# A fused attention and feed-forward kernel on one core: the first weight piece issued by ScalarE, two warm-up matmuls fewer, and re-timed tiles

## The chip, the core and the metric

The kernel runs on one core of one Trainium2 chip. The core has five engines that run side by side, each with its own stream of instructions: TensorE (PE in the profile; its weight loads are shown as PEld), VectorE (DVE), ScalarE (ACT), GpSimd (POOL) and SyncE (SP), which issues most transfers. They wait for each other through semaphores. The metric is device time in microseconds of one execution; several executions are measured and their median is taken.

## The reference

Both halves work on the same x (1 x 2048 x 640, bf16). A is a linear attention with 32 heads of 20; its feature map is a softmax of a small per-head product and of its negative. B is a gated feed-forward net with 1728 hidden columns. A sigmoid gate mixes them.

```python
g = sigmoid((x * gate_w).sum(-1, keepdims=True))
q, k, v = split(x @ wqkv)                       # 32 heads of 20
pq, pk = q @ w_phi, k @ w_phi                   # per head
phi_q = concat([softmax(pq), softmax(-pq)])     # 40 features
phi_k = concat([softmax(pk), softmax(-pk)])
kv, z = phi_k.T @ v, phi_k.sum(over tokens)
a = ((phi_q @ kv) / (phi_q @ z + 1e-6)) @ wo
b = (silu(x @ w_gate) * (x @ w_up)) @ w_down
out = g * a + (1 - g) * b
```

## The kernel before

Everything stays in on-chip memory between load and store. Tokens are handled in four blocks of 512 for the gate and up products and in 16 tiles of 128 for keys, queries and outputs. Products over the 640 input columns are five matmuls of 128 rows each, accumulated in one of eight PSUM banks. x is brought in transposed, by transposing transfers (`load_x`), block by block; block 0 comes in three pieces (columns 0-1, 2-3 and 4 of the five 128-column groups).

The order of work is not written out by hand. Each piece of work is a task for one engine with a cost, dependencies, a priority and the PSUM banks and buffers that it takes (`_Plan.add`). `_Plan.run` (line 286) plays the tasks against the costs and emits the instructions of each engine in the order found; the chip then runs this fixed order, and waits wherever the real times differ. Two sorts of constants steer it:

- `land` in `load` (line 490): the time at which a transfer is taken to have landed. A task that needs it is not placed before that time. Loads of one issuing engine are chained, so that each engine's queue keeps its order.
- `start.hold` (line 880): the earliest planned start of each key tile (`K_AT + K_EACH * t`) and query tile (`Q_AT + Q_EACH * t`). `PRE_Q` is the priority of the products that fold w_phi into the query weights, `D_AFTER` the number of gate-and-up pairs of a block that come ahead of the first down product of the block before.

The start is laid out apart. `warm` (line 614) issues matmuls on a constant into PSUM banks, ten in two groups; nothing reads their results. Behind them `ffn_head` (line 688) computes the first four of the 14 column groups of gate and up for block 0 in pieces, as weights and x arrive: gate over x groups 0-1 for the four column groups (8 matmuls), up over the same (8), then gate and up over x groups 2-4 (12 each). `load_head` (line 537) loads the weight pieces for this. All these loads and the transposing loads of x are issued by SP, one behind the other, beginning with w_gate's piece of two groups by 512 columns. ACT issues one transfer, gate_w, behind its second Tanh; it starts with the load of its function table, ahead of a one-element Tanh.

A key tile runs its products on PE, max, min and two subtractions on DVE, Exp on ACT, sum and reciprocal on DVE and the scaling on POOL. A query tile runs the same and then a transposing transfer, the products with kv, the division on DVE, a second transposing transfer and the product with wo. Gate and up need Tanh and a copy on ACT, one operation on DVE and one on POOL for each column group.

Of the kernel before, what the change touches and what calls it, by code (L numbers as in the profile page):

```python
# [6 lines left out]
P = 128  # L7
# [33 lines left out]
class _Tracker:  # L41
# [123 lines left out]
    def run(self, eng, fn, reads=(), writes=(), semname=None, inc=None):  # L165
        rkeys = [self._key_of(a) for a in reads]
        wkeys = [self._key_of(a) for a in writes]
        need = {}

        def req(ev):  # L170
            if ev is None:
                return
            s, v = ev
            if v > need.get(s, 0):
                need[s] = v

        for k in rkeys:
            for kk in self._conflicts(k):
                req(self.lastw[kk])
        for k in wkeys:  # L180
            for kk in self._conflicts(k):
                req(self.lastw[kk])
                for s, v in self.readers[kk].items():
                    req((s, v))
        self._emit_waits(eng, need)
        ins = fn()
        if semname is None:
            semname = {"pe": "pe", "act": "act", "dve": "dve", "pool": "pool"}[eng]
            if inc is None:
                inc = 1  # L190
        elif semname == "dma":
            semname = self.new_dma_sem()
            inc = 16
        ins.then_inc(self.sem[semname], inc)
        self.cnt[semname] += inc
        v = self.cnt[semname]
        ev = (semname, v)
        snapd = dict(self.known[eng])
        if snapd.get(semname, 0) < v:
            snapd[semname] = v  # L200
        self.evknow.setdefault(semname, {})[v] = snapd
        for k in wkeys:
            self.lastw[k] = ev
            self.readers[k] = {}
        for k in rkeys:
            r = self.readers[k]
            if r.get(semname, 0) < v:
                r[semname] = v
        return ev
# [31 lines left out]
class _Plan:  # L241
# [11 lines left out]
    def add(self, eng, cost, fn, deps=(), prio=5.0, lat=None, acq=(), rel=(), name=""):  # L253
        t = _Task(eng, cost, fn, deps, prio, self.LAT[eng] if lat is None else lat,
                  tuple(acq), tuple(rel), len(self.tasks), name)
        self.tasks.append(t)
        return t
# [86 lines left out]
def _build(  # L344
# [13 lines left out]
    pe, act, dve, pool, sp = nc.tensor, nc.scalar, nc.vector, nc.gpsimd, nc.sync  # L358
# [67 lines left out]
    def one(b, c0, c1, r0=0, r1=P):  # L426
        return ps[r0:r1, b * 512 + c0:b * 512 + c1]
# [42 lines left out]
    def dma(eng, dst, src, transpose=False, keep=False):  # L470
        eobj = tr.engobj[eng]
        reads = [src] if src.tensor.name in tr.addr else []
        writes = [dst] if dst.tensor.name in tr.addr else []
        fn = (lambda: eobj.dma_start(dst, src, transpose=True)) if transpose else (lambda: eobj.dma_start(dst, src))
        ev = run(eng, fn, reads=reads, writes=writes, semname="dma")
        if keep:
            out_evs.append(ev)
# [12 lines left out]
    def load(eng, dst, src, land, prio, transpose=False, name="load", cost=0.06):  # L490

        t = add(eng, cost, lambda: dma(eng, dst, src, transpose=transpose), prio=prio, lat=2.0, name=name)
        t.land = land
        t.slack = L_SLACK if land > 13 else 0.0
        t.after = chain.get(eng)
        chain[eng] = t
        return t
# [7 lines left out]
    wgl = [None] * (NPC + 1)  # L505
    wul = [None] * (NPC + 1)

    def load_gu(j, eng, land, prio):
        c0, c1 = PIECES[j]
        wgl[j] = load(eng, wg[:, :, c0:c1], gsrc[:, :, c0:c1], land[0], prio)  # L510
        wul[j] = load(eng, wu[:, :, c0:c1], usrc[:, :, c0:c1], land[1], prio + 0.1)

    def load_x(bt, prio, *cuts):

        tok = slice(512 * bt, 512 * bt + 512)
        out_ = []
        for i, (c0, c1, land) in enumerate(cuts):
            out_ += [load("sp", xT[:, c0:c1, tok], x2[tok, c0 * P:c1 * P], land, prio + 0.1 * i, True, "x%d" % bt)] * (c1 - c0)
        return out_
# [13 lines left out]
    xs = [None] * NBT  # L533
    HD = 4
    hw = {}

    def load_head(key, c0, c1, k0, k1, land, prio):
        w, src = (wg, gsrc) if key == "g" else (wu, usrc)
        t = load("sp", w[:, c0:c1, k0 * P:k1 * P], src[:, c0:c1, k0 * P:k1 * P], land, prio)
        for k in range(k0, k1):  # L540
            hw[key, c0, k] = t
        return t
    load_head("g", 0, 2, 0, HD, 3.9, -43)
    xa = load_x(0, -42, (0, 2, 5.25))
    load_head("u", 0, 2, 0, HD, 6.9, -41)
    load_head("g", 2, 5, 0, 2, 7.4, -40.5)
    xs[0] = xa + load_x(0, -40, (2, 4, 8.8), (4, 5, 9.3))
    wgl[0] = load_head("g", 2, 5, 2, HD, 10.0, -39.5)
    wul[0] = load_head("u", 2, 5, 0, HD, 11.3, -39)
    load_gu(1, "sp", (12.5, 13.7), -37)  # L550
    xs[1] = load_x(1, -36.5, (0, 5, 16.4))
    phi_rows = A_w_phi.rearrange("h e f -> (h e) f")
# [61 lines left out]
    def warm(banks, before):  # L614
        ctx = {}

        def fn():
            for b in banks:
                last = pe.matmul(one(b, 0, 512), lhsT=ones_row[:, 0:P], rhs=ones_row[:, 0:512], start=True, stop=True, skip_group_check=True)  # L619
            return last  # L620
        b0, b1 = min(banks), max(banks) + 1
        t = add("pe", 0.427 * len(banks), lambda: run("pe", fn, reads=[], writes=[ps[:, b0 * 512:b1 * 512]]), prio=-10,
                acq=[("bank", ctx, i) for i in range(b0, b1)], rel=[("bank", ctx, i) for i in range(b0, b1)], name="warm")
        t.after = before
        return t
    warm_t = warm((4, 5, 6, 7, 4, 5), warm((0, 1, 2, 3), None))


    gate_t = {}
# [85 lines left out]
            ffn_tail(0, k, cs[k], (last["g", k], last["u", k]), 0)  # L715

    B_FIRST = 8
    K_AT, K_EACH, Q_AT, Q_EACH = 29.00, 6.158, 120.27, 8.184
    PRE_Q = 10.11
    PRE_EACH = 2.3  # L720
    PRE_AT = 23.6
    D_AFTER = 5
    FIN_DVE = 12
    K_PAIRS = 9
    store_t = {}
# [64 lines left out]
    def premult(which, wT_l, prio, step=0.0, at=0.0):  # L790
        ev = []
        for m in range(5):
            ctx = {}

            def fn(m=m, ctx=ctx):
                i = ctx["ps"]

                def piece(c, o_, n):
                    k_ = PC if n == PC else P
                    return (o_, wqT[0:k_, NPC_W * which + c, P * m:P * m + P],  # L800
                            wbd[0:k_, c, 0:n // DH, :].rearrange("p k f -> p (k f)"), True, True)
                mms([piece(c, bank(i, 0, 32 + PC * c, 32 + PC * c + PC), PC) for c in range(4)] +
                    [piece(4, bank(i, 1, 0, PC), PC), piece(5, bank(i, 1, PC, PC + 2 * DH), 2 * DH)])
            t1 = add("pe", 0.285, fn, deps=wT_l + wbd_t, prio=prio + step * m, acq=[("pair", ctx, "ps")], name="pre")
            t1.hold = at + PRE_EACH * m if at else 0.0

            def ev_fn(m=m, ctx=ctx):
                i_ = wide(ctx["ps"], 32 + D)[:, 32:32 + D]
                o_ = wkv[:, m, 0:D] if which else wq[:, m, :]
                if which and m % 2:  # L810
                    dveop(lambda: dve.tensor_copy(o_, i_), [i_], [o_])
                else:
                    actop(o_, i_, ACTF.Copy)
            ev.append(add("dve" if which and m % 2 else "act", 0.73 if which and m % 2 else 0.6, ev_fn, deps=[t1], prio=-1,
                          rel=[("pair", ctx, "ps")], name="prev"))
        return ev
# [225 lines left out]
    pre_k = premult(1, wkT_l, 2.0, at=PRE_AT)  # L1042
    pre_q = premult(0, wqT_l, PRE_Q, 0.02)
    wq_done[0] = pre_q[-1]
# [8 lines left out]
    for bt in range(1, NBT):  # L1053
        ks = list(range(K_PAIRS if bt == 1 else 0, NK))
        ds = [("d", u, bt - 1) for u in range(4)]
        for i, k in enumerate(ks):
            seq.append(("f", k, bt))
            if i >= D_AFTER and ds:
                seq.append(ds.pop(0))
# [21 lines left out]
def bass_gated_mix__linear_kernel_hedgehog__swiglu_ffn__prompt_kernel(  # L1081
    nc: bass.Bass,
    A_x: bass.AP,
    A_wqkv: bass.AP,
    A_w_phi: bass.AP,
    A_wo: bass.AP,
    B_x: bass.AP,
    B_w_gate: bass.AP,
    B_w_up: bass.AP,
    B_w_down: bass.AP,  # L1090
    gate_w: bass.AP,
    out: bass.AP,
):
    with nc.Block() as block:
        @block.gpsimd
        def _(g):
            _build(nc, A_x, A_wqkv, A_w_phi, A_wo, B_x, B_w_gate, B_w_up, B_w_down, gate_w, out)
# [29 lines left out]
```

## Time and profile before

| What | us |
|---|---|
| Median of 3 runs (lowest, highest) | 286.96 (286.87, 287.4) |
| The profiled execution | 287.4 |
| Its span, first to last instruction | 285.7 |
| PE busy | 282.5 |
| DVE busy | 223.4 |
| POOL busy | 171.6 |
| ACT busy | 149.1 |
| Transfers, share of 16 DMA engines over the span | 40.1% |

The span is shorter than the execution's time; 1.7 us lie around it. Matmuls are pipelined, and their ends are modelled: one of 512 columns is shown with some 380 ns, while the next starts 216 ns after it. So PE's pace is read from starts, not from lengths. DMA shares are means over short windows and can exceed 1 where packets overlap.

### The profile page before, as it was taken

Reading aid. Unit: us, or ns where it says so; the run is one execution under the profiler, and the core shown is the slowest. Engines: PE = TensorE matmul, PEld = TensorE weight load, DVE = VectorE, ACT = ScalarE, POOL = GpSimd, SP = SyncE. Lnnn points to the kernel's source line nnn. Section 1 sums busy time; section 2 is a strip of 40 time slices with the busy share of each in tenths; the row PEclk is TensorE's granted clock in tenths of the full one; section 3 lists DMA queues with packets and bytes.
Section 4 is the critical chain, followed back from the end, with each engine's and each line's share of the span. In section 5 each row is a group of like instructions: output and inputs, shape, how many; then the busy total and the mean of one; then the engine's idle time right before and its main releaser. Section 6 shows DMA issues by size and latency. Waiting matters only on the chain.

```text
span 285.7 us, 5001 instructions
## 1 busy us (share of the span) xinstructions
PE 282.5 (99%) x1970; PEld 149.6 (52%) x1970; DVE 223.4 (78%) x318; ACT 149.1 (52%) x238; POOL 171.6 (60%) x168
## 2 busy tenths in 40 slices
PE   8999999999999999999999999999999999999996
PEld 3445554555554555654455656555554555555654
DVE  1323449998999797799999999999979979962312
ACT  2455655886676564436636444566664653562210
POOL 5099633749478635456784485589898458638100
PEclk9999999999999999999999999999999999999999
DMA  7979997920000000000002483744375245363211
GB/s 171 271 120 246 214 245 129 334 86 0 0 2 0 0 2 0 2 0 2 0 2 52 76 125 77 109 112 94 69 144 70 55 83 118 70 76 73 71 46 46
DMA packets 68112, 24.22 MB, mean 85 GB/s; under 512 B 56249, under 2 KB 68089, under 8 KB 68089
## 3 DMA queue, kind: packets, MB, share of 16 engines
q1 hardware_dynamic: 67433, 23.91, 40.1%
q8 instruction: 15, 0.25, 0.4%
q10 hardware_dynamic: 656, 0.00, 0.1%
q14 instruction: 8, 0.07, 0.1%
HBM read 8.30 MB, written 2.62 MB: 38 GB/s over the span
## 4 chain that ended last, share of the span: by engine, by line
PE 99%; DVE 0%; issue 0%
PE ps L446 97%; PE ps L619 2%; DVE xsb L749 0%
## 5 line engine op out<-in xcount | busy, mean ns | idle before, releaser
L665 POOL TENSOR_TENSOR hT<-hT,us 128x512 bf16<-128x512 bf16 (+1 forms) x56 | 64.1, 1154 | 53.1 <-DVE hT L659 31.1
L932 POOL TENSOR_TENSOR phi<-phi,rc 128x1320 bf16<-128x1320 bf16 x32 | 77.6, 2426 | 28.8 <-DVE rc L926 26.0
L446 PE MATMUL ps<-xT,wg 128*128 128x512 bf16 x280 | 69.7, 381 | 0.0
L446 PE MATMUL ps<-xT,wu 128*128 128x512 bf16 x260 | 64.3, 379 | 0.0
L446 PE MATMUL ps<-wd,hT 128*128 128x512 bf16 (+1 forms) x448 | 63.0, 299 | 0.0
L922 DVE TENSOR_REDUCE sm<-phi 128x66 f32<-128x1320 bf16 x32 | 48.5, 1519 | 10.6 <-ACT phi L456 10.6
L659 DVE SCALAR_TENSOR_TENSOR hT<-hT,ps 128x512 bf16<-128x512 bf16 (+1 forms) x56 | 37.6, 676 | 22.8 <-ACT hT L456 22.7
L456 ACT ACTIVATE hT<-ps 128x512 bf16<-128x512 f32 (+1 forms) x56 | 33.2, 597 | 40.7 <-PE ps L446 40.3
L456 ACT ACTIVATE phi<-phi 128x1320 bf16<-128x1320 bf16 x32 | 41.7, 1304 | 22.2 <-DVE phi L911 22.2
L446 PEld LDWEIGHTS ps<-wd,hT 128*128 128x128 bf16 x448 | 35.0, 98 | 27.4
L446 PE MATMUL ps<-wkv,xT 128*128 128x289 bf16 (+2 forms) x240 | 45.8, 343 | 0.0
L456 ACT ACTIVATE us<-ps 128x512 bf16<-128x512 f32 (+1 forms) x56 | 33.2, 597 | 16.4 <-PE ps L446 14.2
L446 PEld LDWEIGHTS ps<-xT,wu 128*128 128x128 bf16 x260 | 25.3, 98 | 30.8 <-ACT phi L456 0.4
L446 PEld LDWEIGHTS ps<-xT,wg 128*128 128x128 bf16 x280 | 26.0, 98 | 27.9 <-issue 1.5
L446 PEld LDWEIGHTS ps<-wkv,xT 128*128 128x128 bf16 x240 | 22.9, 97 | 18.4
L899 DVE TENSOR_REDUCE mx<-ps 128x33 f32<-128x660 f32 x32 | 26.6, 833 | 3.4 <-PE ps L446 3.3
L911 DVE TENSOR_TENSOR phi<-mn,ps 128x660 bf16<-128x660 f32 x32 | 26.4, 824 | 0.3
L903 DVE TENSOR_REDUCE mn<-ps 128x33 f32<-128x660 f32 x32 | 26.5, 828 | 0.0
L907 DVE TENSOR_TENSOR phi<-ps,mx 128x660 bf16<-128x660 f32 x32 | 26.5, 827 | 0.0
L456 ACT ACTIVATE xsb<-ps,gs 128x640 bf16<-128x640 f32 x16 | 12.7, 793 | 24.7 <-PE ps L446 24.7
L446 PE MATMUL ps<-wq,xT 128*128 128x512 bf16 (+1 forms) x160 | 24.3, 299 | 0.0
L446 PE MATMUL ps<-wo,oT 128*128 128x512 bf16 (+1 forms) x160 | 24.3, 299 | 0.0
(47 smaller groups left out, 184.9 us busy)
## 6 DMA issues: line engine op xcount, KB each, us to landing
out_dram<-xsb SPq DMA_DIRECT2D x15, 160.0 KB, 1.8
wd<-in_B_w_down_dram SPq DMA_DIRECT2D x1, 2080.0 KB, 9.3
wg<-in_B_w_gate_dram SPq DMA_DIRECT2D x2, 400.0 KB, 5.3
wu<-in_B_w_up_dram SPq DMA_DIRECT2D x2, 400.0 KB, 6.5
wo<-in_A_wo_dram SPq DMA_DIRECT2D x1, 800.0 KB, 10.0
wg<-in_B_w_gate_dram SPq DMA_DIRECT2D x2, 320.0 KB, 4.7
wu<-in_B_w_up_dram SPq DMA_DIRECT2D x2, 320.0 KB, 5.6
wkv<-in_A_wqkv_dram SPq DMA_DIRECT2D x1, 600.0 KB, 4.4
```

The source lines that it names most:

```text
L446: last = pe.matmul(o, lhsT=l, rhs=r, start=st, stop=sp_, skip_group_check=True)
L456: run("act", lambda: act.activation(o, i, func, scale=scale), reads=reads, writes=[o])
L619: last = pe.matmul(one(b, 0, 512), lhsT=ones_row[:, 0:P], rhs=ones_row[:, 0:512], start=True, stop=True, skip_group_check=True)
L659: dveop(lambda: dve.scalar_tensor_tensor(out=hap, in0=hap, scalar=1.0, in1=g_, op0=ALU.add, op1=ALU.mult), [hap, g_], [hap])
L665: poolop(lambda: pool.tensor_tensor(hap, hap, u_, ALU.mult), [hap, u_], [hap])
L899: dveop(lambda: dve.tensor_reduce(a, b, AX.X, ALU.max), [b], [a])
L903: dveop(lambda: dve.tensor_reduce(a, b, AX.X, ALU.min), [b], [a])
L907: dveop(lambda: dve.tensor_tensor(o_, a, b, ALU.subtract), [a, mx[:, ctx["st"], :]], [o_])
L911: dveop(lambda: dve.tensor_tensor(o_, a, b, ALU.subtract), [b, mn[:, ctx["st"], :]], [o_])
L922: dveop(lambda: dve.tensor_reduce(a, b, AX.X, ALU.add), [b], [a])
L932: poolop(lambda: pool.tensor_tensor(a, a, b, ALU.mult), [a, r], [a])
```

## The change

The first piece of w_gate is issued by ACT and no longer by SP, through a new argument of `load_head`. SP's queue then begins with the first piece of x. The planned landing times of the head's pieces become smaller. The second group of warm-up matmuls has four in place of six. Five constants of the planned order are changed: key tiles are planned 0.05 us further apart, query tiles start 1.25 us earlier and lie 0.097 us closer, `PRE_Q` goes from 10.11 to 10.14 and `D_AFTER` from 5 to 4. No computation of the result is changed.

```diff
-    def load_head(key, c0, c1, k0, k1, land, prio):
+    def load_head(key, c0, c1, k0, k1, land, prio, eng="sp"):
         w, src = (wg, gsrc) if key == "g" else (wu, usrc)
-        t = load("sp", w[:, c0:c1, k0 * P:k1 * P], src[:, c0:c1, k0 * P:k1 * P], land, prio)
+        t = load(eng, w[:, c0:c1, k0 * P:k1 * P], src[:, c0:c1, k0 * P:k1 * P], land, prio)
         for k in range(k0, k1):
             hw[key, c0, k] = t
         return t
-    load_head("g", 0, 2, 0, HD, 3.9, -43)
-    xa = load_x(0, -42, (0, 2, 5.25))
-    load_head("u", 0, 2, 0, HD, 6.9, -41)
-    load_head("g", 2, 5, 0, 2, 7.4, -40.5)
-    xs[0] = xa + load_x(0, -40, (2, 4, 8.8), (4, 5, 9.3))
-    wgl[0] = load_head("g", 2, 5, 2, HD, 10.0, -39.5)
-    wul[0] = load_head("u", 2, 5, 0, HD, 11.3, -39)
+    load_head("g", 0, 2, 0, HD, 3.9, -43, "act")
+    xa = load_x(0, -42, (0, 2, 4.6))
+    load_head("u", 0, 2, 0, HD, 6.2, -41)
+    load_head("g", 2, 5, 0, 2, 6.9, -40.5)
+    xs[0] = xa + load_x(0, -40, (2, 4, 8.0), (4, 5, 8.5))
+    wgl[0] = load_head("g", 2, 5, 2, HD, 9.6, -39.5)
+    wul[0] = load_head("u", 2, 5, 0, HD, 10.9, -39)
...
-    warm_t = warm((4, 5, 6, 7, 4, 5), warm((0, 1, 2, 3), None))
+    warm_t = warm((4, 5, 6, 7), warm((0, 1, 2, 3), None))
...
-    K_AT, K_EACH, Q_AT, Q_EACH = 29.00, 6.158, 120.27, 8.184
-    PRE_Q = 10.11
+    K_AT, K_EACH, Q_AT, Q_EACH = 29.00, 6.208, 119.02, 8.087
+    PRE_Q = 10.14
...
-    D_AFTER = 5
+    D_AFTER = 4
```

## The prediction

> **What bounds the kernel now.** I read the page's busy shares first, then the chain of work that ended last.
>
> ```profile
> PE 282.5 (99%) x1970; PEld 149.6 (52%) x1970; DVE 223.4 (78%) x318; ACT 149.1 (52%) x238; POOL 171.6 (60%) x168
> ...
> PE ps L446 97%; PE ps L619 2%; DVE xsb L749 0%
> ```
>
> TensorE (PE) is busy for 99% of the span, and the chain is PE nearly from end to end. A busy PE need not be a PE at its pace, so next I looked at the starts of single matmuls. In the steady part a 512-column matmul starts 0.216 us after the one before it, and that pace is hardly ever broken. The largest break I found is this one:
>
> ```profile
> 137.34 1.03 PE L446 MATMUL ps<-xT,wg 128*128 128x512 bf16 x4
> 138.25 0.59 PE L446 MATMUL ps<-xT,wu 128*128 128x512 bf16 x2
> ```
>
> Four matmuls at 0.216 from 137.34 end at 138.20; the next begins at 138.25, 0.05 late. The excess over the pace, summed over all starts from 6.34 on, is about 0.2 us. So the end is set by three things: when PE begins useful work, at which pace it runs there, and whether anything makes it wait later. Third view, the timeline of the first microseconds (start, length, engine) of SyncE (SP), of PE and of PE's weight loads (PEld), which mark single matmul starts:
>
> ```profile
> 0.80 0.46 SPq L474 DMA_DIRECT2D wg<-in_B_w_gate_dram  x1
> 1.32 1.32 SPq L474 DMA_TRANSPOSE xT<-in_A_x_dram  x1
> 2.70 0.56 SPq L474 DMA_DIRECT2D wu<-in_B_w_up_dram  x1
> ```
>
> ```profile
> 0.84 4.43 PE L619 MATMUL ps<-const-bfloat16-1.0 128*128 128x512 bf16 x10 [0.84 <-PEq L1111]
> 5.08 2.50 PE L446 MATMUL ps<-xT,wg 128*128 128x512 bf16 x8
> 7.42 1.89 PE L446 MATMUL ps<-xT,wu 128*128 128x512 bf16 x8
> ```
>
> ```profile
> 5.05 0.16 PEld L446 LDWEIGHTS ps<-xT,wg 128*128 128x128 bf16 x2 [0.69 <-issue]
> 5.49 0.15 PEld L446 LDWEIGHTS ps<-xT,wg 128*128 128x128 bf16 x1 [0.28 <-issue]
> 5.92 0.15 PEld L446 LDWEIGHTS ps<-xT,wg 128*128 128x128 bf16 x1 [0.28 <-issue]
> 6.34 0.75 PEld L446 LDWEIGHTS ps<-xT,wg 128*128 128x128 bf16 x4 [0.27 <-issue]
> ```
>
> Ten warm-up matmuls cover 0.84 to 5.06; the first useful one starts at 5.08. Up to 6.34 starts lie 0.427 us apart, after it 0.216: the clock turns at about 6.33. The views of transfers (median us from issue to landing) and of ScalarE (ACT) for the same stretch:
>
> ```profile
> wg<-in_B_w_gate_dram SPq DMA_DIRECT2D x1, 256.0 KB, 3.0
> xT<-in_A_x_dram SPq DMA_TRANSPOSE x1, 3.6
> ```
>
> ```profile
> 0.80 1.28 ACT L456 ACT_TABLE_LOAD   x1 [0.80 <-PEq L1111]
> ...
> 10.64 0.60 ACT L456 ACTIVATE hT<-ps 128x512 bf16<-128x512 f32 x1 [8.34 <-PE ps L446]
> ```
>
> The first piece of x lands at 1.32 + 3.6 = 4.9, just ahead of 5.05; w_gate lands at 0.80 + 3.0 = 3.8.
>
> **The change, part by part.**
>
> *Warm-ups.* Two of ten go, so PE is free at 0.84 + 8 x 0.424 = 4.23 (ten took 4.24). From there it waits for x and w_gate, if they are not there.
>
> *Issue.* ACT issues w_gate's piece at 0.80; its cost is 0.46 (SP's row). ACT's table load moves from 0.80 to 1.26 and its first Tanh from 2.09 to about 2.55, hidden under the 8.34 us in which ACT waits for PE up to 10.64; without that cover it would cost 0.46. SP issues x at 0.80, not 1.32, and what follows on SP's queue moves up by up to 0.52. Both transfers now run side by side. Windows of the trace (columns: window, length, busy time of each engine with counts, clock, DMA share, GB/s):
>
> ```profile
> 1.80:3.10 1.30, 1.30 (x5) 0.46 (x4) 0.68 (x3) 0.49 (x2) 1.09 (x5) 1.00 0.73 195
> 3.10:3.90 0.80, 0.80 (x4) 0.27 (x2) 0.54 (x2) 0.00 (x0) 0.70 (x3) 1.00 1.19 240
> ```
>
> The DMA engines have room only up to 3.1 (share 0.73). So x lands between 0.52 earlier (all of the issue time) and not earlier (the same 512 KB through the same full engines), and w_gate no later than the pair together, 4.9. I take 0.40: nearer the full value, because the room lies where x's packets would now begin. PE's first useful matmul is then at 5.08 - 0.40 = 4.68. The Trainium skill, DMA: Bandwidth & Descriptors, "Issuing engines are not separate DMA queues", says that issuing from several engines saves only the sequencer's issue time, since the same 16 engines move everything. By it the gain is at most the 0.52 and may be nothing, which is rival B; the DMA shares above agree.
>
> *What an earlier start is worth.* The clock turns at a time, 6.33, and what PE does ahead of it runs at half pace: 1 us more gives 1/0.427 = 2.34 matmuls, each of which saves 0.216 later, 0.51 us. So 0.40 x 0.51 = -0.20. Bounds: 0, and -0.43 (two matmuls at 0.216) if both transfers were there at 4.23.
>
> *The rest of the head.* w_up's piece lands at 2.70 + 3.3 = 6.0 and is needed at 7.42 - 0.20 = 7.22; the second and third piece of x land at 8.0 and 8.5 by their semaphores and are needed 0.20 before 9.15 and 10.01. Even if none came earlier, they have about 1 us; with that gone PE would wait microsecond for microsecond. Cost nothing.
>
> *The order behind.* K_EACH, Q_AT, Q_EACH, PRE_Q and D_AFTER move the planned starts. The order of the built program shows the same work on each engine, apart from the two matmuls and the moved issue, but PE, VectorE (DVE), ACT and SyncE come in another order from the first key tiles on. The work costs nothing; the waits are redrawn. From below: the 0.2 us of excess goes. From above, VectorE: it is full where the query tiles run (same columns; the third busy time is DVE's):
>
> ```profile
> 121.00:150.00 29.00, 29.00 (x215) 15.12 (x214) 28.79 (x40) 13.96 (x23) 20.77 (x17) 1.00 0.01 1
> 150.00:200.00 50.00, 50.00 (x389) 27.57 (x388) 49.12 (x74) 27.35 (x34) 33.97 (x29) 1.00 0.50 92
> ```
>
> Query tiles are planned 8.184 - 8.087 = 0.097 closer; if DVE takes none of that and PE waits for it each time, 16 x 0.097 = +1.55. I take +0.20: four breaks of the size of the one at 138.25, nearer the lower bound because PE's waits now end that close to the pace, and the new order has no more work to place.
>
> *The end* is as before: the last stores follow the last matmul in the same order, 283.3 to 285.7.
>
> Sum: -0.20 + 0.20 = 0.0. The span stays 285.7 and its execution 287.4 (1.7 lies around the span). That execution is the slowest of the three shown, 0.44 above their median of 286.96, so the forecast is **287.0**. 0.2%, 0.57 us, is about what a measurement of this kernel can tell from no change.
>
> **Rivals.**
>
> A, faster: the clock turns before the useful matmuls start, and each microsecond counts in full. x lands 0.52 earlier, the 0.2 of excess shrinks to 0.1: 286.96 - 0.52 - 0.1 = 286.3. For it: the other runs are 0.44 and 0.53 faster than the profiled one, as a clock that turns 1 us earlier would make them (1 x 0.51). Against it: in the one execution that shows the clock it turned 1.25 us after the first useful start.
>
> B, the change doesn't do what it says: x lands at 4.9 as before. PE idles from 4.23, nothing is gained, the redrawn waits stay: 287.2.
>
> C, slower, at one place: the hole in PE's work from 4.23 to 4.68 makes the clock begin anew. Before, the clock turned 6.33 - 0.84 = 5.49 after the first matmul, with no hole. Counted from 4.68 it turns at 10.17, and PE runs 3.84 us longer at half pace: 3.84 x 0.51 = +1.9, so 288.9. It decides as soon as the granted clock turns after about 6.4. For it: the one turn that the trace shows came with no hole ahead of it. Against it: the hole is 0.45 of 5.49 us. The Trainium skill, TensorE: Matmul & The Clock Gate, "Part 1", names a free-running window of about 3.4 us that must be busy; by it a hole could cost at most one window, an estimated 3.4 x 0.51 = 1.7 us. No row here shows how much idleness is allowed.
>
> D, slower: DVE sets the pace among the query tiles. Ten of the 16 at 0.097 cost 1.0: 288.0. For it: 28.79 busy of 29.00. Against it: DVE has no more work than before, and has 43 - 39.5 = 3.5 us free between 200 and 243.
>
> **Chances.** The forecast (286.6 to 287.4) 0.36, A 0.25, B 0.09, C 0.13, D 0.17. The range 286.3 to 288.1 leaves out C and the lower quarter of A, about 0.19. Faster by over 0.2%: most of A (0.22) and the forecast's edge (0.03), 0.25. Slower: C, most of D (0.15) and the other edge (0.03), 0.31. Within: 0.44.
>
> **What would show it.** Eight warm-ups ending at 4.23; x landing near 4.5 and the first useful matmul near 4.7 (5.08 shows B); the change from 0.427 to 0.216 near 6.3 (10 shows C, below 4.7 shows A); then four cold useful matmuls in place of three; the steady pace with about 0.4 us of breaks in all (1 us or more, with PE released by DVE between 120 and 245, shows D). A landing of w_up after 7.2, or a tail over 2.4 us, would be a miss that no case holds.

## The result, and the profile after

| | Before | After |
|---|---|---|
| Median of 22 runs each, us | 287.10 | 287.66 |
| Lowest, highest | 286.71, 287.65 | 287.33, 289.56 |
| Mean | 287.11 | 287.89 |
| The profiled execution | 287.4 | 289.38 |
| Its span | 285.7 | 287.7 |

The ratio after to before is 1.0026, with an interval of 1.0016 to 1.0037: slower, by about what such a measurement can tell. The means are 0.78 apart and the medians 0.56. The 22 runs after are not one heap. Nineteen lie between 287.33 and 287.98, with a mean of 287.65; three lie at 289.27, 289.38 and 289.56. The profiled execution is one of these three, so its profile shows a loss that most executions don't have. The two parts have to be read apart.

The page of the kernel after, first the busy time of each engine, then the shares of the chain of waits by engine and by line:

```profile
PE 283.6 (99%) x1968; PEld 149.6 (52%) x1968; DVE 224.1 (78%) x318; ACT 150.3 (52%) x238; POOL 171.5 (60%) x168
...
PE 96%; DMA 1%; ACT 1%; DVE 0%; issue 0%
PE ps L446 96%; DMA xT<-in_A_x_dram 1%; ACT phi L456 0%; ACT hT L456 0%; ACT us L456 0%; DVE xsb L749 0%
```

PE still shows 99%. New on the chain are a transfer of x at its head, and ACT with 1%. The head comes first: the timelines of SP, of PE and of PE's weight loads (start, length, engine, line, what was done).

```profile
0.80 1.33 SPq L474 DMA_TRANSPOSE xT<-in_A_x_dram  x1
2.19 0.57 SPq L474 DMA_DIRECT2D wu<-in_B_w_up_dram  x1
```

```profile
0.84 3.57 PE L619 MATMUL ps<-const-bfloat16-1.0 128*128 128x512 bf16 x8 [0.84 <-PEq L1111]
5.21 3.57 PE L446 MATMUL ps<-xT,wg 128*128 128x512 bf16 x8 [0.79 <-DMA xT<-in_A_x_dram]
```

```profile
5.18 0.14 PEld L446 LDWEIGHTS ps<-xT,wg 128*128 128x128 bf16 x2 [1.67 <-issue]
5.59 0.15 PEld L446 LDWEIGHTS ps<-xT,wg 128*128 128x128 bf16 x1 [0.28 <-issue]
...
9.00 0.15 PEld L446 LDWEIGHTS ps<-xT,wu 128*128 128x128 bf16 x1 [0.27 <-issue]
9.41 0.96 PEld L446 LDWEIGHTS ps<-xT,wu 128*128 128x128 bf16 x5 [0.26 <-issue]
```

SP begins with x at 0.80, 0.52 earlier than before, but the first useful matmul starts at 5.21, 0.13 later than before. Weight loads go on 0.42 apart up to 9.41, and then five of them take 0.96: the clock turns there, not at 6.33. The clock column of the windows prints 1.00 here as well as in the stretch before the turn that the prediction shows, because the trace's clock records begin with the turn (at 9.378 here, at 6.333 before) and time ahead of them is counted as full; so the pace is read from the starts. The view of transfers (KB, us from issue to landing) shows why x brought nothing here:

```profile
wg<-in_B_w_gate_dram ACTq DMA_DIRECT2D x1, 256.0 KB, 3.1
xT<-in_A_x_dram SPq DMA_TRANSPOSE x1, 4.3
```

x took 3.6 from issue to landing before and takes 4.3 now. The chain of waits, in order of time, shows what is new late in the span:

```profile
200.45 1.19 ACT phi L456
201.64 0.02 issue
201.66 0.60 ACT hT L456
202.26 0.49 ACT us L456
202.76 0.05 issue
202.81 82.50 PE ps L446 x613
```

PE waits at 202.81 for a copy of ACT, "us", which stands behind an Exp ("phi") and another copy. Before, ACT had no Exp at this place and waited for PE, not PE for ACT:

```profile
200.39 0.60 ACT L456 ACTIVATE hT<-ps 128x512 bf16<-128x512 f32 x1
201.31 0.60 ACT L456 ACTIVATE us<-ps 128x512 bf16<-128x512 f32 x1 [0.32 <-PE ps L446]
```

The starts of PE show two more breaks of the pace, at 81.20 and 150.47, and none of note elsewhere. The timeline of all engines around each:

```profile
80.38 0.30 ACT L846 ACTIVATE gs<-gtan 128x4 f32<-128x4 f32 x2
...
80.59 0.55 ACT L456 ACTIVATE v<-ps 128x480 bf16<-128x480 f32 x1
...
81.19 0.76 PEld L446 LDWEIGHTS ps<-xT,wg 128*128 128x128 bf16 x5 [0.42 <-ACT v L456]
...
149.17 0.57 DVE L979 TENSOR_TENSOR ps<-ps,kvm 128x384 f32<-128x384 f32 x1
149.77 0.56 DVE L980 TENSOR_TENSOR kvsb<-ps,kvacc 128x384 bf16<-128x384 f32 x1
...
150.47 0.74 PE L446 MATMUL ps<-v,phi 128*128 128x64 bf16 x20
```

At 81.20 the gate product needs the bank that ACT's copy of v empties; that copy stands behind the two small scalings "gs". At 150.47 the product with v waits for two operations of DVE. Measured against the steady pace (0.216 a matmul of 512 columns, 0.056 one of 128) the three breaks are 0.10, 0.15 and 0.22, together 0.47. Before there was one, of 0.05.

These three differences close the profiled execution. The first useful start is 0.13 later. Ten matmuls run at half pace, (9.41 - 5.21) / 0.42, in place of three, and each costs 0.427 - 0.216 = 0.211, so 7 x 0.211 = 1.48. The breaks add 0.47 - 0.05 = 0.42. The sum is 2.03; the spans differ by 2.0.

### The profile page after: what moved, and what is told of

Same layout as the page of the kernel before. It is cut to its first block, busy times and chain, and to the rows that moved or that the text cites. A ratio compares the mean times of both kernels' runs of the same rounds, so it can differ in the third digit from the quotient of the medians.

```text
span 287.7 us, 5016 instructions
## 1 busy us (share of the span) xinstructions
PE 283.6 (99%) x1968; PEld 149.6 (52%) x1968; DVE 224.1 (78%) x318; ACT 150.3 (52%) x238; POOL 171.5 (60%) x168
## 4 chain that ended last, share of the span: by engine, by line
PE 96%; DMA 1%; ACT 1%; DVE 0%; issue 0%
PE ps L446 96%; DMA xT<-in_A_x_dram 1%; ACT phi L456 0%; ACT hT L456 0%; ACT us L456 0%; DVE xsb L749 0%
## 5 line engine op out<-in xcount | busy, mean ns | idle before, releaser
L446 PE MATMUL ps<-xT,wg 128*128 128x512 bf16 x280 | 70.6, 386 | 0.8 <-DMA xT<-in_A_x_dram 0.8
```

What stands on the lines that cost most here:

```text
L446: last = pe.matmul(o, lhsT=l, rhs=r, start=st, stop=sp_, skip_group_check=True)
```

## The experiments

The theory going in: the new order costs some 0.4, the head brings nothing where x lands no earlier, and the late clock is a matter of the hole in PE's work. The rivals: the loss is in the head, or the late clock comes by chance. So the order and the head are taken apart. To keep all else in place, a task can be planned on one engine and issued by another, and a group of warm-ups can be planned longer or shorter than it runs:

```diff
-    def load(eng, dst, src, land, prio, transpose=False, name="load", cost=0.06):
+    def load(eng, dst, src, land, prio, transpose=False, name="load", cost=0.06, via=None):
...
-        t = add(eng, cost, lambda: dma(eng, dst, src, transpose=transpose), prio=prio, lat=2.0, name=name)
+        t = add(eng, cost, lambda: dma(via or eng, dst, src, transpose=transpose), prio=prio, lat=2.0, name=name)
...
-    def warm(banks, before):
+    def warm(banks, before, planned=None):
...
-        t = add("pe", 0.427 * len(banks), ...
+        t = add("pe", 0.427 * (planned or len(banks)), ...
```

`load_head` takes such an engine as its last argument and hands it on as `via`. All ratios are to the kernel before, run on the same chip in between.

**plan_only: the order alone.** The changed kernel with its new order; SP issues w_gate as before, and ten warm-ups run.

```diff
-    load_head("g", 0, 2, 0, HD, 3.9, -43, "act")
+    load_head("g", 0, 2, 0, HD, 3.9, -43, "act", "sp")
...
-    warm_t = warm((4, 5, 6, 7), warm((0, 1, 2, 3), None))
+    warm_t = warm((4, 5, 6, 7, 4, 5), warm((0, 1, 2, 3), None), 4)
```

> The order of the changed kernel with the head of the kernel before: SyncE issues w_gate's piece again, ten warm-ups. Theory P (the redrawn order costs the time: its starts exceed the pace by 0.64 us outside the cold part, before by 0.21): +0.4 us over before, 1.0014, with PE late by 0.1 to 0.2 us near 81, 150 and 202 us; no run near +2 us. Theory H (the hole in PE's work ahead of the first useful matmul costs it, through the clock): no difference, 1.000. Theory T (the transfers of the head are slower when two engines issue): no difference, 1.000.

Measured: 287.47 (287.15 to 288.07), ratio 1.0013 (1.0004 to 1.0022), +0.37. The three breaks are there, at the same instructions: 0.106 at 78.98, 0.144 at 148.26 and 0.219 at 200.58. PE's timeline (start, length) around the last:

```profile
199.29 1.24 PE L446 MATMUL ps<-xT,wg 128*128 128x512 bf16 x5
200.58 0.61 PE L446 MATMUL ps<-xT,wu 128*128 128x512 bf16 x2
```

From 199.29 five matmuls at 0.216 take up to 200.37, and the next begins 0.21 later; before, there was no such wait there. The breaks sum to 0.47, 0.42 more than before, and the time is 0.37 higher: the order is a loss by itself. It takes in the five constants and the planned landing times of the head; which of them makes the breaks was not taken apart.

**after_warm10: the changed kernel with ten warm-ups**, its order kept.

```diff
-    warm_t = warm((4, 5, 6, 7), warm((0, 1, 2, 3), None))
+    warm_t = warm((4, 5, 6, 7, 4, 5), warm((0, 1, 2, 3), None), 4)
```

> The changed kernel with ten warm-ups, planned as eight, so that no other instruction moves: the hole from 4.2 to 5.2 us is filled. Theory P: still +0.4 us over before in the median, 1.0014, but no run near +2 us. Theory H: back to before, 1.000. Theory T: as the changed kernel, +0.5.

Measured: 287.45 (287.14 to 288.05), 1.0014 (1.0006 to 1.0023), with the three breaks. No run is late. Without a hole, and with ACT's issue, the order's loss is what remains.

**head_only: the head alone.** The kernel before, in its own order, with ACT's issue and eight warm-ups planned as ten. It ran three times, the last two on another chip than the first.

```diff
-    load_head("g", 0, 2, 0, HD, 3.9, -43)
+    load_head("g", 0, 2, 0, HD, 3.9, -43, "act")
...
-    warm_t = warm((4, 5, 6, 7, 4, 5), warm((0, 1, 2, 3), None))
+    warm_t = warm((4, 5, 6, 7), warm((0, 1, 2, 3), None), 6)
```

> The order of the kernel before with the head of the changed one: ScalarE issues w_gate's piece, eight warm-ups, planned as before, so that no other instruction moves. Theory P: the median within 0.15 us of before, 1.000; x lands near 5.0, PE idle from 4.2. Theory H: +0.5 us in the median, 1.0018, and some runs near +2 us. Theory T: +0.3 to +0.5 us, with x or w_up landing later than before.

> The order of before with the head of the changed kernel once more, for the share of late runs, of which the first 11 runs had none. Theory C (the hole of about 1 us makes the clock turn late in some executions, as in 3 of 12 with the warm-up cut alone and 3 of 22 of the changed kernel): 1 to 4 of some 11 runs 1.5 to 2.2 us above the others. Theory A (with ScalarE issuing there is no late run unless the new order is there too): none.

> The head of the changed kernel in the order of before, the third time, as the version that may beat both (0.9996 and 0.9988 of before in the first two). Theory P: 0.9985 to 1.0 of before, 0.35 to 0.45 us below the changed kernel. Theory H: 1.001 to 1.002 of before.

Measured: ratios 0.9996 (0.9988 to 1.0005), 0.9988 (0.9978 to 0.9997) and 0.9991 (0.9980 to 1.0002), in mean 0.9992, -0.24 us. None of the 34 runs is late. x landed at 4.83, 4.58 and 4.63. What an earlier x brings is partly given back. PE's timeline of the second:

```profile
4.71 1.89 PE L446 MATMUL ps<-xT,wg 128*128 128x512 bf16 x8 [0.30 <-DMA xT<-in_A_x_dram]
6.80 1.90 PE L446 MATMUL ps<-xT,wu 128*128 128x512 bf16 x8 [0.20 <-DMA wu<-in_B_w_up_dram]
...
10.29 1.47 PE L446 MATMUL ps<-xT,wg 128*128 128x512 bf16 x6 [0.29 <-DMA wg<-in_B_w_gate_dram]
```

Eight matmuls from 4.71 at full pace are through at 6.43, so PE waits 0.37 for w_up's piece; later it waits 0.46 for w_gate's. A faster head runs into its next transfers. It is still the best of the variants: no break of the order but the one of 0.05.

**issue_only: ACT's issue with ten warm-ups.**

```diff
-    load_head("g", 0, 2, 0, HD, 3.9, -43)
+    load_head("g", 0, 2, 0, HD, 3.9, -43, "act")
```

> The kernel before with w_gate's piece issued by ScalarE and nothing else changed, ten warm-ups. Theory P: within 0.1 us of before, x lands at 4.9 to 5.1 although it is issued 0.52 us earlier. Theory H: the same as before. Theory T: +0.3 to +0.5 us. Had the full issue time been gained, x would land at 4.4 and PE would still be held by the ten warm-ups up to 5.06.

Measured: 286.98 (286.64 to 287.62), 0.9995 (0.9986 to 1.0004). x landed at 5.06, later than in the profiled execution before (4.95), though it was issued 0.52 earlier. The issue alone changes nothing that can be measured.

**warm8_only and warm6_only: fewer warm-ups alone**, SP issuing w_gate. This makes the hole that rival C needs, and widens it.

```diff
-    warm_t = warm((4, 5, 6, 7, 4, 5), warm((0, 1, 2, 3), None))
+    warm_t = warm((4, 5, 6, 7), warm((0, 1, 2, 3), None), 6)
...
-    warm_t = warm((4, 5, 6, 7, 4, 5), warm((0, 1, 2, 3), None))
+    warm_t = warm((4, 5), warm((0, 1, 2, 3), None), 6)
```

> The kernel before with eight warm-ups, planned as ten, SyncE issuing as before: a hole in PE's work from 4.2 to about 5.0 us and nothing else. Theory C (a hole makes the clock turn late in some executions): the median within 0.1 us of before, and about 1 run in 7 some 1.6 to 2.2 us above it. Theory N (the late runs of the changed kernel have another cause, in the order behind or in the transfers): no run more than 0.8 us above the median.

> The kernel before with six warm-ups, planned as ten: a hole from 3.4 to about 5.0 us. Theory C: more late runs than with eight warm-ups, a third or more, each 1.3 to 2.2 us above before. Theory N: as before, no late run; the median within 0.1 us.

Measured with eight: 287.25 in median; nine runs at 286.99 to 287.55 and three at 288.87, 288.92 and 288.95; ratio 1.0017 (1.0001 to 1.0033). With six: 288.69 in median; three runs at 286.77 to 287.12 and nine at 288.17 to 289.86; 1.0037 (1.0017 to 1.0057). The profile with six, PE's weight loads:

```profile
4.90 0.14 PEld L446 LDWEIGHTS ps<-xT,wg 128*128 128x128 bf16 x2 [2.25 <-issue]
...
10.01 0.15 PEld L446 LDWEIGHTS ps<-xT,wu 128*128 128x128 bf16 x1 [0.28 <-issue]
10.31 0.31 PEld L446 LDWEIGHTS ps<-xT,wu 128*128 128x128 bf16 x2 [0.16 <-issue]
```

The loads lie 0.43 apart up to 10.01 and 0.30 at 10.31, so the clock turns at about 10.2. The two heaps thus come with fewer warm-ups alone, without the order or ACT's issue, and the late share grows with the hole: 0 of 130 runs of the kernel before, 3 of 12 with a hole of about 1.0 (5.19 - 4.2), 9 of 12 with about 1.5 (4.93 - 3.4). The hole of a single run is known only where it was profiled, so these holes stand for their kernels. The profiled execution with eight is one of the nine: its clock turned at 3.48, ahead of its hole.

**x_first: is x late because w_gate is beside it?** w_gate's issue is placed behind ACT's first Tanh, so that x should have the DMA engines for itself.

```diff
-    load_head("g", 0, 2, 0, HD, 3.9, -43)
+    first = load_head("g", 0, 2, 0, HD, 3.9, -43, "act")
+    go_first, first.fn = first.fn, lambda: None
...
-    table = add("act", 1.3, lambda: actop(us[:, 1, 0:1], us[:, 0, 0:1], ACTF.Tanh), deps=[zero], prio=-20, name="table")
+    table = add("act", 1.3, lambda: (actop(us[:, 1, 0:1], us[:, 0, 0:1], ACTF.Tanh), go_first()), deps=[zero], prio=-20, name="table")
```

> The kernel before with SyncE beginning with x, and w_gate's piece issued by ScalarE only behind its table load and Tanh, near 2.3 us, so that no transfer is ahead of x or beside it at its start. Theory S (x was held by w_gate's packets on the same engines): x lands at 3.7 to 4.0 us, as the transposing transfers of wqkv do (3.1 us from issue). Theory L (a transposing transfer of this size takes that long from its issue whatever runs beside it): x lands at 4.7 us or later. In both, w_gate comes near 5.3 and PE starts useful work near 5.4.

Measured: 287.04 in one run, 0.1 under the median of the kernel before. The condition was missed: ACT issued w_gate at 0.98, in the middle of its table load and not behind it. The order of the packets did change. Those of x began at 2.2 and those of w_gate at 2.6, where x's had begun at 2.8 to 2.9 behind w_gate's.

```profile
wg<-in_B_w_gate_dram ACTq DMA_DIRECT2D x1, 256.0 KB, 3.7
```

w_gate landed at 0.98 + 3.7 = 4.7, x at 5.21. The one that goes first gains nothing for the pair.

**split_head: halves.** Since the pair sets the start, PE could begin with half of it. x and w_gate come in two pieces each, w_up from ACT, and the first useful matmuls go by column group.

```diff
+    first.fn = lambda: [dma("act", wg[:, c:c + 1, 0:HD * P], gsrc[:, c:c + 1, 0:HD * P]) for c in range(2)]
...
+    xa[0].fn = lambda: [dma("sp", xT[:, c:c + 1, 0:512], x2[0:512, c * P:c * P + P], transpose=True) for c in range(2)]
...
+    go_up = lambda: dma("act", wu[:, 0:2, 0:HD * P], usrc[:, 0:2, 0:HD * P])
```

> A version meant to be faster than both: the order of the kernel before, w_gate's first piece cut in two and issued by ScalarE, x's first piece cut in two and issued first by SyncE, w_up's piece issued by ScalarE behind its table load, eight warm-ups; the first eight useful matmuls run over the first column group of x, then over the second. Theory S: the half pieces land near 4.0, PE starts useful work near 4.2 and is 0.8 us earlier, worth 0.4 us at half pace and more where the clock has turned: 0.9985. Theory L: the halves land after 4.5, and the gain is under 0.2 us: 0.9995.

Measured: 287.07 (286.83 to 287.50), 0.9994 (0.9986 to 1.0003). PE's weight loads:

```profile
4.35 0.14 PEld L446 LDWEIGHTS ps<-xT,wg 128*128 128x128 bf16 x2 [0.84 <-issue]
4.71 0.32 PEld L446 LDWEIGHTS ps<-xT,wg 128*128 128x128 bf16 x2 [0.22 <-issue]
5.83 0.56 PEld L446 LDWEIGHTS ps<-xT,wg 128*128 128x128 bf16 x4 [0.81 <-issue]
...
9.94 0.98 PEld L446 LDWEIGHTS ps<-xT,wg 128*128 128x128 bf16 x6 [0.47 <-DMA wg<-in_B_w_gate_dram]
```

The first half of x lands at 4.24 and PE starts at 4.38, but after four matmuls it stands from about 5.36 to 5.86, since the second half lands at 5.73. Further waits follow up to 11. The head is bound by its transfers: of a start 0.7 earlier than before no gain is left that can be told from none.

**three_waits_cut: are the breaks the loss?** plan_only with what stands ahead of each late instruction made short: the scalings of block 1 are made with those of block 2, the Exp of query tile 8 and the sum of query tile 0 run over 1 of 11 groups.

```diff
+                q = slice(4 * bt - 4 if bt == 2 else 4 * bt, 4 * bt + 4)
+                for w, a in ((0, 0.5), (1, -0.5)) if bt != 1 else ():
...
+        x1 = add("act", 1.2, lambda: actop(*[dst()[:, 0:1 if (t, which) == (8, 0) else NG, :]] * 2, ACTF.Exp), ...
...
+            n = 1 if (t, which) == (0, 0) else NG
```

> The order of the changed kernel with the head of the kernel before, as in the run with the order alone, and work taken away just ahead of three waits of PE: the two small gate scalings of token block 1 (ScalarE, ahead of the copy of v near 80 us) go with those of block 2; the sum over the features of query tile 0 (VectorE, ahead of the masked kv of the last block near 147) runs over one of its 11 groups; the Exp of query tile 8 (ScalarE, ahead of the copy of up near 200) runs over one of 11 groups. The rest of these two tiles' features is left out. Theory P (these three waits are what the new order costs): the breaks of 0.10, 0.15 and 0.22 us near 79, 148 and 200 go, and the time is 0.3 to 0.45 us below the order alone: 0.9998 to 1.0003 of before. Theory M (the cost is spread, or such waits come back at the next place): at least half of it stays, 1.0007 or more.

Measured: 287.07 (286.91 to 287.48), 1.0001 (0.9992 to 1.0010). The breaks at 79 and 200 are gone, the one at 148 stays at 0.145. The timeline of all engines there:

```profile
146.18 0.86 PE L446 MATMUL ps<-v,phi 128*128 128x64 bf16 x24
...
147.08 0.57 DVE L981 TENSOR_TENSOR ps<-ps,kvm 128x384 f32<-128x384 f32 x1 [1.20 <-PE ps L446]
147.09 1.31 PE L446 MATMUL ps<-wq,xT 128*128 128x512 bf16 x9
...
147.68 0.56 DVE L982 TENSOR_TENSOR kvsb<-ps,kvacc 128x384 bf16<-128x384 f32 x1
...
148.38 0.74 PE L446 MATMUL ps<-v,phi 128*128 128x64 bf16 x20
```

With the sum cut short DVE stood idle for 1.20 and waited for PE. So this break is no queue on DVE, as had been supposed: it is a round trip from PE's product through two operations of DVE (0.57 + 0.56) back to PE, with too few matmuls in between to cover it. In the profile of the change 1.51 lie between the end of that product (148.97) and 150.47, and the ten matmuls in between fill 1.36 of it. The other two breaks, 0.106 + 0.219 = 0.325, went, and the loss went from 0.37 to 0.03. That agrees, within intervals of about 0.26 each way.

**after_2: the changed kernel once more**, beside head_only_3 on one chip. No edit.

> The changed kernel once more, on the same chip and beside the same runs of before as its own head with the order of before. Theory P: the order costs 0.4 us, so that it is 0.35 to 0.45 us above the kernel with the head alone; 0 to 3 late runs of some 11, by how early x lands on this chip. Theory H (the head of the changed kernel costs the time): no difference between the two.

Measured: 287.37 (286.89 to 287.83), 1.0009 (1.0000 to 1.0019), no late run among 12. x landed at 4.63, the first useful matmul started at 4.76, the clock turned at 5.54; the breaks are 0.103, 0.145 and 0.220. head_only_3 beside it measured 286.76, 0.61 less: the same head with the old order. That is more than the 0.35 to 0.45 of Theory P; each ratio has an interval of about 0.3 us either way.

## Why the prediction was right or wrong

The forecast was 287.0, the median is 287.66. It lies within the range of 286.3 to 288.1, but above the forecast's own 286.6 to 287.4. The likeliest case, no change, did not come: the ratio says slower.

**The order: the step that was mis-sized.** It stood as "I take +0.20: four breaks of the size of the one at 138.25". The runs show three breaks of 0.10, 0.15 and 0.22, 0.42 more than before, and +0.37 and +0.40 in time with the new order and no hole. What failed was to take the size of a new break from an old one. A break's size is how late the releaser is, and that depends on what the new order puts ahead of it: an Exp of 1.29 between ACT's copies in one place, a round trip of 1.51 with ten matmuls of 1.36 to cover it in another. The reason given, that the new order has no more work to place, says nothing on that.

**Rival D, DVE as the pace,** had the sign, not the mechanism. DVE is no fuller after (columns as before, the third busy time is DVE's):

```profile
121.00:150.00 29.00, 29.00 (x228) 15.79 (x226) 27.79 (x37) 14.44 (x24) 17.64 (x16) 1.00 0.00 1
150.00:200.00 50.00, 50.00 (x386) 27.26 (x385) 49.02 (x74) 25.27 (x33) 34.60 (x28) 1.00 0.43 82
```

It was 28.79 and 49.12. Two of the three releasers are ACT, and there are three single places, not a loss at each query tile.

**The head: right in mean, for part of its reasons.** Forecast -0.20; the head alone measured -0.24 in the mean of three calls. The step "I take 0.40" for x was too much, and at 0.51 a microsecond the 0.16 measured would be worth only -0.08, so that the two numbers meet is partly luck. In the five profiles in which SP issues w_gate ahead of x (before, plan_only, three_waits_cut, warm8_only, warm6_only), x landed at 4.80 to 5.14, in mean 4.95; in the seven in which ACT issues it beside x (the change, after_2, after_warm10, issue_only and the three of head_only), at 4.58 to 5.08, in mean 4.79. That is 0.16 earlier for an issue 0.52 earlier, with a spread wider than the gain; the profiled execution of the change, at 5.08, is rival B itself. The reason given was that the room lies where x's packets would now begin. They did not begin there: the first packet of x went at 2.77 to 2.93 in the seven, behind the first of w_gate's at 1.9, and at 2.79 to 3.00 in the five. The windows had shown the bound, full DMA engines. The Trainium skill, DMA: Bandwidth & Descriptors, "Issuing engines are not separate DMA queues", says that issue from several engines saves at most the issue time; the 0.16 for 0.52 agrees. "Cost nothing" for the rest of the head was wrong: w_up's piece landed at 6.28 to 7.24 in the seven, in mean 6.70, though it was issued 0.5 earlier than in the five (5.97 to 6.93, in mean 6.39). The 6.0 that the forecast took from one profile was the earliest of the five. The 7.24, in the profile of the change, is past the 7.2 that the prediction had named as a miss that no case holds; it cost nothing there, since PE came to this product only at 8.58. In the second head_only PE waited 0.37 for this piece and 0.46 for w_gate's.

**Rival C happened, in some executions.** Three of 34 runs of the changed kernel are late, and the profile of one shows the clock's turn at 9.38. The price was near: 1.9 forecast, 289.40 - 287.65 = 1.75 measured between the means of the two heaps. The point from which it decides held also, as 9.38 is past 6.4. The count behind it did not: 5.49 after the first useful start would have been 10.70, and the clock turned 4.17 after it. What the forecast lacked is that it is no yes or no: it comes in a share of the executions that grows with the hole. So the median hardly has it, and the mean has 3 / 22 x 1.75 = 0.24 of it. The Trainium skill, TensorE: Matmul & The Clock Gate, "Part 1", describes a free-running window of about 3.4 us, which gave an estimate of at most 1.7; the 1.75 is close to it, the 1.99 between the heaps with six warm-ups is above it, and a turn that falls at other times in other executions agrees.

**Rival A's premise came, without its whole price.** In the profiles of plan_only and head_only the clock had turned before the first useful matmul. That is a matter of the execution more than of the change, as the last section shows. In the second head_only the head then ran at full pace into its next transfers, with the two waits above, and that execution took 287.24. The third had no such wait and took 286.50, against 286.70 for the fastest run of before beside it: 0.2, not 0.6.

The account of the 22 runs: the mean is 0.78 higher. Of this 0.24 is the late turn and some 0.38 the order. The 0.16 that is left is not explained; it is less than the 0.3 that the interval of the ratio reaches either way.

Open in part: why the changed kernel had 3 late runs in 22 and then none in 12, and head_only none in 34 with the same eight warm-ups. The holes in the profiles fit (about 1.0 in the late profile, 0.5 to 0.75 in after_2 and the first two of head_only), and the last section shows which holes matter. That x landed late in just the late runs is argued, not shown: only one of them was profiled.

## What to carry to other kernels

On an engine that is busy for 99%, look at starts against the steady pace, and for each planned wait ask what stands ahead of its releaser in that engine's queue: 0.47 us of breaks did not show in the busy share. Change an order and a head apart from each other: here the head alone (0.9992 in mean) is 0.6 us better than head and order together on the same chip. Take warm-up work away only as far as the useful work closes up to it, and read all the runs and not the median alone, because a share of late executions is a cost that a median hides.

## What the runs showed of the hardware

The clock's turn is no fixed time. With ten warm-ups it came at 6.33 in the kernel before; in plan_only the ten took 4.02 where they took 4.43 before, so the last ones ran at full pace and it came at about 4.3. Those 2.0 us are worth 2.0 x 0.51 = 1.0 us, about the spread of the runs of one kernel (286.71 to 287.65).

The trace's clock records tell more. Eight of the 14 profiles hold one that begins with the turn. It lasts 279.89 us in five of them (before, the change, after_2, after_warm10, x_first) and 283.31 in three (the third head_only, three_waits_cut, warm8_only). The difference is 3.41, and the two are 82 and 83 times that. So the turn falls on marks 3.41 apart, and where these marks lie in the span differs from execution to execution. The table counts how long PE stood idle, ahead of the first matmul or in the hole, in the 3.41 that end at the turn and in the 3.41 before those.

| Profile | Turn, us | Idle in the 3.41 that end there | Idle in the 3.41 before |
|---|---|---|---|
| before | 6.33 | 0.02 | 1.34 |
| the change | 9.38 | 0.00 | 1.00 |
| after_2 | 5.54 | 0.55 | 2.13 |
| the third head_only | 3.53 | 0.73 | all |
| warm8_only | 3.48 | 0.77 | all |
| warm6_only (turn from the starts) | 10.2 | 0.00 | 1.57 |

In these the clock turned at the end of the first such stretch in which PE was idle for 0.77 or less. Stretches with 1.00 or more did not turn it, nor did one with about 0.9 (warm6_only, up to 3.35). By this a hole makes an execution late when it leaves too much idle time in the stretch that would otherwise have turned the clock; in warm8_only's profile the hole came behind the turn, and its 1.3 cost no pace. This is worked out from the profiles afterwards: no run places the marks or sets the idle time by itself.

The 512 KB of x and w_gate were both there at 4.6 to 5.2, whichever was issued first and from whichever engine, and the next piece, issued 0.5 earlier, landed no earlier (w_up at 6.70 in the mean of the seven profiles with ACT's issue, at 6.39 in that of the five with SP's).

A transfer issued by ACT did not wait for ACT's table load: issue at 0.98, load from 0.80 to about 2.1.
